# A two-layer decode kernel: the last two heads of each round written apart, two more wo pieces loaded last in round one, ReLU into two PSUM banks

## The chip, the cores and the metric

The kernel runs on one core of a Trainium2 chip. The metric is the device time of one execution in microseconds (us); the time before is the median of three runs. The profile is of one further execution on the same kind of core.

## The reference

Four sequences (B = 4) decode one token. A residual stream x of 4 x 640 goes twice through the same two layers, so the kernel has two rounds:

```python
x = x + _A_ref(_layernorm(x), k_cache, v_cache, wq, wo)   # 32 heads of 128, the last 1024 keys
x = x + _B_ref(_layernorm(x), w1, w2)                     # relu(x @ w1) @ w2, 1728 hidden
x = x + _A_ref(_layernorm(x), k_cache, v_cache, wq, wo)
x = x + _B_ref(_layernorm(x), w1, w2)
```

In `_A_ref` each head computes q = x wq, scores q k / sqrt(128), a softmax over 1024 keys, p v, and adds its part times wo. Everything is float32. Nothing can be shared between the sequences in the attention, since each has its own cache, so per round all keys and values of 32 heads are read once.

## The kernel before, in words

**Data.** The host packs one *record* per head, 128 partitions x 9472 columns: wq (640 columns), keys (4096), values (4096), wo (640) at the column offsets WQ, K, V, WO (line 47). A record is 4.85 MB. It is loaded into one of five SBUF buffers, `slot0` to `slot4`; a sixth buffer, `ring`, holds w1 and w2 of round one and then parts of the first records of round two. Heads 27 to 31 stay in the five slots at the end of round one, and round two begins with them, so that they are read from HBM once.

**Order of the transfers.** All loads go to the SP queue in one list, `items`, built at lines 180 to 216. `pump` (line 218) issues the head of the list as soon as nothing live overlaps its columns; `done` (line 239) frees columns when PE's last use of them has been written down in the program. `ending` (line 170) cuts the records of the last three heads a, b, c of a round into pieces: query weights and keys of a and b, values of a, keys of c, values of b, the values of c in two halves. In round one the three wo pieces of a, b, c are loaded behind all of these (lines 175 to 177, LATE = 3 at line 68), then the five blocks of w1 and seven pieces of w2. The second piece of w2 lies on the columns of the first block of w1, so it cannot be issued before PE has read that block; the same holds for the pieces after it.

**The work of a head** (lines 391 to 405). The engines' programs are written down in order, and each engine runs its own list in that order:
- `query` (291): five 128 x 128 products into the PSUM tile misc, copied by DVE to qT.
- `scores` (298): eight products of 512 columns into sc_ps[s], two banks of PSUM; s alternates by head. DVE takes the maximum, ACT the exponential with its sum.
- `weights` (311): DVE turns that sum into a factor, and transposes and scales the two halves of the exponentials into wT, one after the other.
- `values` (321): eight products of 512 columns, four for each half of the keys, into o_ps, one bank; then DVE picks the right block of each sequence out of o_ps in four operations, into `on`.
- `output_T` (332): PE transposes `on` into the same o_ps, DVE copies it to oTs.
- `project` (336): four products with wo, added into acc.

The loop writes scores of head n+1, then values of head n, the query of head n+2, output and projection of head n, and weights of head n+1. For the last `late` heads of a round (3 in round one, 1 in round two) the projection stands after the loop (lines 406 to 411), because their wo comes last; the last head's output is transposed there too, behind two fillers. A *filler* is `busy(n)` (line 256), a product of n columns into one row of a bank, whose result nobody reads.

**The MLP** (343). `center` (260) makes the layernorm's mean with fillers in between. w1 is multiplied in five blocks into h_ps, the first bank of sc_ps[0], again with fillers. DVE clears 32 columns of h_ps, ACT applies ReLU in three pieces within that bank, and DVE transposes the two halves to `scratch` (355 to 362). The w2 products go into acc tile by tile; the first 28 of the 54 tiles use only the first transposed half.

Of the kernel before, what the change touches and what calls it, by code (L numbers as in the profile page):

```python
# [33 lines left out]
AF = mybir.ActivationFunctionType  # L34
OP = mybir.AluOpType
# [4 lines left out]
B, D, H, DH, W, FF = 4, 640, 32, 128, 1024, 1728  # L40
# [6 lines left out]
WQ, K, V, WO = 0, D, D + 4 * W, D + 8 * W  # L47
REC = 2 * D + 8 * W
# [4 lines left out]
FQ = FF // NB  # L53
# [11 lines left out]
           (7808, 8320, 0)]  # L65
W1_SLOT = [[0, 1], [2], [3], [4]]
W2_SLOT = [22, 20, 8, 4]
LATE = 3


class InOrder:
# [21 lines left out]
def decode_kernel(ctx: ExitStack, tc: tile.TileContext, xf, rec, w1, w2, out):  # L93
    nc = tc.nc
    pe, dve, act, pool, sp = (InOrder(tc, e) for e in (nc.tensor, nc.vector, nc.scalar, nc.gpsimd, nc.sync))
# [3 lines left out]
    mean_of = sb.tile([P, P], F32, name="mean_of")  # L99
    xT = sb.tile([P, FD], F32, name="xT")  # L100
    scratch = sb.tile([P, 480], F32, name="scratch")
    wT = scratch[:, :128].rearrange("p (i c j) -> p i c j", i=2, c=16)
    on = scratch[:, 128:256]
    xc = scratch[:, 256:256 + FD]
    x_sb = scratch[:, :FD]
    spread = scratch[:, 256:288]
    hT = scratch.rearrange("p (m j) -> p m j", j=32)
    oTs = sb.tile([P, LATE, B], F32, name="oTs")
    qT = sb.tile([P, B], F32, name="qT")
    of_batch = sb.tile([P, B], F32, name="of_batch")  # L110
    of_block = sb.tile([P, 4], F32, name="of_block")
    pick = sb.tile([P, B], F32, name="pick")
    mrt = sb.tile([P, B], F32, name="mrt")
    small = sb.tile([P, 12], F32, name="small")
    nmax, rtot, rstd, eps, eps_dh, ones, unused, sums, squares, tot0, tot1 = (small[:, i:i + 1] for i in range(11))
    tot = [tot0, tot1]
    slot = [sb.tile([P, REC], F32, name=f"slot{i}") for i in range(NS)]
    ring = sb.tile([P, RING], F32, name="ring")

    sc_ps = [ps.tile([P, W], F32, name=f"sc_ps{i}") for i in range(2)]  # L120
    t_ps = ps.tile([P, 512], F32, name="t_ps")
    o_ps = ps.tile([P, 512], F32, name="o_ps")
    acc = ps.tile([P, 512], F32, name="acc")
    misc = ps.tile([P, 512], F32, name="misc")

    dve.memset(x_sb, 0.0)
    for n in range(NB):
# [25 lines left out]
    LAST = H - NS  # L153

    def home(h, r):

        return h % NS if not r or h >= LAST else (h - 6 + LAST) % NS
# [6 lines left out]
    def load(key, src, lo, hi, buf, col):  # L164
        items.append((key, src, lo, hi, buf, col))

    def piece(r, h, lo, hi, buf=None, col=None):
        load(("rec", r, h), rec[h], lo, hi, home(h, r) if buf is None else buf, lo if col is None else col)

    def ending(r, hs, late):  # L170
        a, b, c = hs[-3:]
        end = WO if late else REC
        for h, lo, hi in ((a, 0, V), (b, 0, V), (a, V, end), (c, 0, V), (b, V, end), (c, V, V + VH), (c, V + VH, end)):
            piece(r, h, lo, hi)
        if late:
            for h in hs[-3:]:
                piece(r, h, WO, REC)


    hs = order[0]  # L180
    piece(0, hs[0], 0, V)
    piece(0, hs[0], V, REC)
    for h in hs[1:-3]:
        piece(0, h, 0, REC)
    ending(0, hs, True)
    for k, col in enumerate(W1_RING):
        load(("w1", 0), w1, k * FF, k * FF + FF, "ring", col)
    n = 0
# [5 lines left out]
    hs = order[1]  # L194
# [18 lines left out]
    n = 0  # L213
# [39 lines left out]
        pump()  # L253


    def busy(n):

        pe.matmul(sc_ps[1][0:1, :n], mean_of[:, 0:1], slot[home(LAST, 0)][:, K:K + n], start=True, stop=True)

    def center(fill):  # L260

# [26 lines left out]
    def xblock(k):  # L288
        return xT[:, 32 * k:32 * k + B]

    def query(r, h):
        key = ("rec", r, h)
        for k in range(KB):
            pe.matmul(misc[:, 8:8 + B], cols(key, WQ + k * DH, DH), xblock(k), start=(k == 0), stop=(k == KB - 1))
        done(key, WQ, K)
        dve.tensor_copy(qT, misc[:, 8:8 + B])

    def scores(r, h, s, first=False):
        key = ("rec", r, h)
        for i in range(2):  # L300
            for b in range(B):
                pe.matmul(sc_ps[s][32 * b:32 * b + 4, 512 * i:512 * i + 512], qT[:, b:b + 1].to_broadcast([P, 4]),
                          cols(key, K + 512 * (B * i + b), 512), start=True, stop=True)
            done(key, K + VH * i, K + VH * i + VH)
        dve.tensor_reduce(nmax, sc_ps[s], op=OP.max, axis=AX.X, negate=True)
        if first:
            dve.reciprocal(rstd, rstd)
        dve.tensor_tensor(nmax, nmax, rstd, op=OP.mult)
        act.activation(sc_ps[s], sc_ps[s], AF.Exp, bias=nmax, scale=rstd, accum_out=tot[s])

    def weights(s):

        dve.transpose(spread, tot[s].to_broadcast([P, 32]))
        dve.reciprocal(rtot, spread[:, 0:1])
        dve.tensor_scalar(mrt, of_batch, rtot, None, op0=OP.mult)
        for i in range(2):
            dve.transpose(t_ps, sc_ps[s][:, 512 * i:512 * i + 512])
            dve.tensor_tensor(wT[:, i], t_ps.rearrange("p (c j) -> p c j", j=32)[:, :, :B],
                              mrt.unsqueeze(1).to_broadcast([P, 16, B]), op=OP.mult)

    def values(r, h):
        key = ("rec", r, h)
        for i in range(2):
            for g in range(4):
                pe.matmul(o_ps[32 * g:32 * g + 16, :], wT[:, i, 4 * g:4 * g + 4, :].rearrange("p c j -> p (c j)"),
                          cols(key, V + VH * i + 512 * g, 512), start=(i == 0), stop=(i == 1))
            done(key, V + VH * i, V + VH * i + VH)
        dve.tensor_scalar(on, o_ps[:, :DH], of_block[:, 0:1], None, op0=OP.mult)
        for c in range(1, 4):
            dve.scalar_tensor_tensor(on, o_ps[:, DH * c:DH * c + DH], of_block[:, c:c + 1], on, op0=OP.mult, op1=OP.add)  # L330

    def output_T(i):
        pe.matmul(o_ps[:, :B], on, pick, start=True, stop=True)
        dve.tensor_copy(oTs[:, i], o_ps[:, :B])

    def project(r, h, i, end):
        key = ("rec", r, h)
# [3 lines left out]
        done(key, WO, REC)  # L341

    def mlp(r):
        h_ps = sc_ps[0][:, :512]
        for k in range(KB):
            for j in range(NB):
                pe.matmul(h_ps[32 * j:32 * j + B, :FQ], xblock(k), cols(("w1", r), k * FF + FQ * j, FQ),
                          start=(k == 0), stop=(k == KB - 1))
            done(("w1", r), k * FF, k * FF + FF)
            if k == 0:  # L350
                scale_hidden()
            elif k < KB - 1:
                busy(512)

        dve.memset(h_ps[:, FQ:FQ + 32], 0.0)
        act.activation(h_ps[:, :224], h_ps[:, :224], AF.Relu, scale=rstd)
        act.activation(h_ps[:, 464:480], h_ps[:, 416:FQ], AF.Relu, scale=rstd)
        act.activation(h_ps[:, 224:FQ], h_ps[:, 224:FQ], AF.Relu, scale=rstd)
        busy(512)
        busy(256)  # L360
        dve.transpose(scratch[:, :224], h_ps[:, :224])
        dve.transpose(scratch[:, 224:], h_ps[:, 224:480])
        key = ("w2", r)
        sizes = W2_SLOT if r else [size for size, _ in W2_RING]
        first = 0
        for i, size in enumerate(sizes):
            for s in range(first, first + size):
                m, n = TILES[s]
                w = cols(key, s * FD, FD)
                for part, q in ((m, n),) if m < 13 else ((13, n), (14, n + 2)):  # L370
                    pe.matmul(acc[32 * q:32 * q + B, :FD], hT[:, part, :B], w,
                              start=False, stop=(s >= len(TILES) - NB), skip_group_check=True)
            for _ in range((i < len(sizes) - 1, 2 * (i == 0))[r]):
                busy(512)
            done(key, first * FD, (first + size) * FD)
            first += size
# [3 lines left out]
    pe.matmul(acc[:, :FD], ident, x_sb, start=True, stop=False, skip_group_check=True)  # L380
    for r in range(2):
        hs = order[r]
        late = LATE if r == 0 else 1
        center(r > 0)
        dve.tensor_scalar(mrt, mean_of[:, :B], squares, None, op0=OP.mult)
        query(r, hs[0])
        scale_scores()
        scores(r, hs[0], 0, True)
        query(r, hs[1])
        weights(0)  # L390
        for n, h in enumerate(hs):
            more = n + 1 < H
            i = n - (H - late)
            if more:
                scores(r, hs[n + 1], (n + 1) % 2)
            values(r, h)
            if n + 2 < H:
                query(r, hs[n + 2])
            if i < 0:
                output_T(0)  # L400
                project(r, h, 0, False)
            elif more:
                output_T(i)
            if more:
                weights((n + 1) % 2)
        for i in range(late):
            if i == max(0, late - 2):
                busy(512)
                busy(512)
                output_T(late - 1)  # L410
            project(r, hs[H - late + i], i, i == late - 1)
        center(True)
        mlp(r)
# [40 lines left out]
```

## Time and profile before

| | before |
|---|---|
| median of three runs | 727.33 us (726.65 to 728.99) |
| the profiled execution | 727.87 us, its span 726.2 us |
| transfers | 304.49 MB, mean 419 GB/s |
| PE (matmul) busy | 526.8 us, 73% |
| DVE busy | 357.2 us, 49% |
| ACT busy | 96.0 us, 13% |
| mean granted clock of TensorE | 0.788 |

Times in the rows below are us from the span's start. PE is TensorE's matmuls, PEld its weight loads, DVE VectorE, ACT ScalarE, SPq the queue of SyncE that issues the transfers. In a timeline row stand start, duration, engine, line, operation, out<-in, shapes and count; a float32 matmul shows as two. Since a helper records every instruction, all rows have the line L85, and one goes by the tiles' names. The bracket at the end of a row is the idle time of the engine before it and what ended it.

### The profile page before, as it was taken

What the parts mean: (1) busy time and instruction counts of PE and PEld (TensorE: products, weight loads), DVE (VectorE), ACT (ScalarE), POOL (GpSimd) and SP (SyncE); (2) the same over time, 40 slices, a digit from 0 to 9 for tenths busy, and PEclk for the clock granted to TensorE, in tenths of its full rate; (3) what the DMA queues carried; (4) which work ended last, traced back from release to release, by engine and by line L of the source; (5) the groups of instructions that cost most, each with busy time, mean ns of one, the idle gap of its engine ahead of it and who ended that gap; (6) DMA issues with size and microseconds to landing.
All of it is one profiled execution on the core that took longest, in us unless ns stands there. A gap on an engine that the chain in (4) does not pass through costs nothing.

```text
span 726.2 us, 8920 instructions
## 1 busy us (share of the span) xinstructions
PE 526.8 (73%) x3712; PEld 213.4 (29%) x3712; DVE 357.2 (49%) x1000; ACT 96.0 (13%) x154; POOL 1.1 (0%) x9
## 2 busy tenths in 40 slices
PE   3466768677767586668889889675767767768888
PEld 2132322323313232233324343233222232323412
DVE  3344445444454445445732777653444544544750
ACT  2101011010110101101211221210101010110201
POOL 0000000000000000000000000000000000000000
PEclk9778776776687868767999898977787886766969
DMA  9999999999999999999999999999999999999994
GB/s 385 430 425 429 432 433 433 435 431 431 432 431 432 429 431 428 427 427 426 419 361 405 394 423 429 436 430 433 431 432 431 433 430 427 434 429 420 423 422 205
DMA packets 15336, 304.49 MB, mean 419 GB/s; under 512 B 1712, under 2 KB 1984, under 8 KB 5312
## 3 DMA queue, kind: packets, MB, share of 16 engines
q1 hardware_dynamic: 15264, 303.91, 98.3%
q8 instruction: 29, 0.48, 0.3%
q14 instruction: 11, 0.09, 0.0%
q10 hardware_dynamic: 32, 0.01, 0.0%
HBM read 303.84 MB, written 0.08 MB: 419 GB/s over the span
## 4 chain that ended last, share of the span: by engine, by line
DMA 74%; PE 20%; DVE 4%; issue 1%; ACT 0%; SPq 0%
DMA slot<-rec 74%; PE sc_ps L85 8%; PE o_ps L85 5%; PE misc L85 4%; PE acc L85 4%; DVE scratch L85 2%; DVE oTs L85 1%; ACT sc_ps L85 0%; DVE small L85 0%; DVE t_ps L85 0%; SPq L85 0%; DVE mrt L85 0%; SPq L82 0%; DVE sc_ps L85 0%; DVE qT L85 0%
## 5 line engine op out<-in xcount | busy, mean ns | idle before, releaser
L85 PE MATMUL misc<-xT,slot 128*128 128x4 f32 x620 | 102.8, 293 | 154.9 <-DMA slot<-rec 154.0
L85 PE MATMUL sc_ps<-slot,qT 128*4 128x512 f32 x992 | 196.7, 934 | 0.8 <-DVE qT L85 0.7
L85 PEld LDWEIGHTS misc<-xT,slot 128*128 128x128 f32 x620 | 97.4, 242 | 210.7 <-DMA slot<-rec 199.1
L85 ACT ACTIVATE sc_ps<-sc_ps,small 128x1024 f32<-128x1024 f32 (+3 forms) x70 | 77.5, 1107 | 571.8 <-DVE small L85 546.7
L85 PE MATMUL o_ps<-slot,scratch 128*16 128x512 f32 x1010 | 140.1, 673 | 4.3 <-DVE scratch L85 3.5
L85 DVE TENSOR_REDUCE small<-sc_ps 128x1 f32<-128x1024 f32 x64 | 78.2, 1223 | 79.2 <-PE sc_ps L85 79.2
L85 DVE STREAM_TRANSPOSE t_ps<-sc_ps 128x512 f32<-128x512 f32 x128 | 93.2, 728 | 2.2
L85 DVE COPY qT<-misc 128x4 f32<-128x4 f32 x64 | 10.2, 159 | 167.5 <-PE misc L85 167.5
L85 PEld LDWEIGHTS o_ps<-slot,scratch 128*16 128x16 f32 x1010 | 34.1, 117 | 132.2 <-issue 81.2
L85 DVE SCALAR_TENSOR_TENSOR scratch<-o_ps,of_block,scratch 128x128 f32<-128x128 f32 x192 | 67.3, 350 | 6.8
L85 PEld LDWEIGHTS sc_ps<-slot,qT 128*4 128x4 f32 x992 | 33.8, 116 | 84.8 <-issue 74.3
L85 PE MATMUL acc<-slot,oTs 128*4 128x160 f32 x512 | 39.1, 390 | 15.5 <-DVE oTs L85 15.5
L85 DVE TENSOR_SCALAR scratch<-o_ps,of_block 128x128 f32<-128x128 f32 x64 | 22.4, 350 | 38.0 <-PE o_ps L85 38.0
L85 PE MATMUL o_ps<-pick,scratch 128*128 128x4 f32 x128 | 29.4, 300 | 9.4 <-DVE scratch L85 9.4
L85 DVE TENSOR_TENSOR scratch<-t_ps,mrt 128x64 f32<-128x64 f32 x128 | 28.8, 225 | 4.4
L85 PEld LDWEIGHTS o_ps<-pick,scratch 128*128 128x128 f32 x128 | 26.1, 253 | 14.3 <-DVE scratch L85 13.3
L85 PE MATMUL sc_ps<-slot,mean_of 128*1 128x512 f32 (+1 forms) x62 | 28.9, 571 | 0.0
L85 DVE COPY oTs<-o_ps 128x4 f32<-128x4 f32 x64 | 10.4, 162 | 18.6 <-PE o_ps L85 17.5
L85 DVE TENSOR_SCALAR mrt<-of_batch,small 128x4 f32<-128x4 f32 x64 | 14.7, 230 | 2.2
L85 PEld LDWEIGHTS acc<-slot,oTs 128*4 128x4 f32 x512 | 7.3, 84 | 22.1 <-DVE oTs L85 21.0
L85 DVE STREAM_TRANSPOSE scratch<-small 128x32 f32<-128x32 f32 x64 | 12.9, 201 | 1.4 <-ACT sc_ps L85 1.4
L85 ACT ACTIVATION_READ_ACCUMULATOR sc_ps<-sc_ps,small 128x1 f32 x64 | 12.2, 191 | 0.0
(55 smaller groups left out, 104.4 us busy)
## 6 DMA issues: line engine op xcount, KB each, us to landing
slot<-rec SPq DMA_DIRECT2D x46, 4736.0 KB, 30.8
slot<-rec SPq DMA_DIRECT2D x17, 2368.0 KB, 16.9
slot<-rec SPq DMA_DIRECT2D x5, 1024.0 KB, 32.4
ring<-w SPq DMA_DIRECT2D x5, 864.0 KB, 13.6
slot<-rec SPq DMA_DIRECT2D x2, 2048.0 KB, 42.8
slot<-rec SPq DMA_DIRECT2D x3, 1344.0 KB
slot<-w SPq DMA_DIRECT2D x3, 864.0 KB, 31.2
ring<-rec SPq DMA_DIRECT2D x1, 2368.0 KB
```

Source lines behind the costliest of these rows:

```text
L85: r = build(*args, **kwargs)
```

## The change

1. **Loads.** LATE is 5: in round one the wo pieces of the last five heads, not of the last three, come behind the last values. Heads 27 and 28 lose their 640 wo columns in their first load, and two loads of 640 columns are added ahead of the other three.
2. **Last two heads apart.** The loop stops at the third head from the end. Then come the scores of the last head, the values of the head before it, the *weights* of the last head, the picks of the head before it, the values of the last head, its picks. The last head's values, output and picks use a second bank, the upper half of sc_ps[0], and a second `on`.
3. **Fillers.** The two fillers of 512 columns behind the last values go. After each half of the values of the last head but one stands one filler, after each half of the last head's values two, all into misc.
4. **Projections.** In round one five projections stand after the loop, three of them without a transposition between; in round two there are two instead of one.
5. **ReLU.** The first piece goes to t_ps, the other two to the upper bank of sc_ps[0], in the order 208 columns, 16 columns. The memset of the gap stands at the start of the MLP.

```diff
-LATE = 3
+LATE = 5
-    on = scratch[:, 128:256]
+    on = [scratch[:, 128:256], scratch[:, 288:416]]
+    outs = [o_ps, sc_ps[0][:, 512:]]
-            for h in hs[-3:]:
+            for h in hs[-LATE:]:
                 piece(r, h, WO, REC)
-        piece(0, h, 0, REC)
+        piece(0, h, 0, REC if h < H - LATE else WO)
...
-    def values(r, h):
+    def values(r, h, last=False, fill=0):
         key = ("rec", r, h)
         for i in range(2):
             for g in range(4):
-                pe.matmul(o_ps[32 * g:32 * g + 16, :], wT[:, i, 4 * g:4 * g + 4, :].rearrange("p c j -> p (c j)"),
+                pe.matmul(outs[last][32 * g:32 * g + 16, :], wT[:, i, 4 * g:4 * g + 4, :].rearrange("p c j -> p (c j)"),
                           cols(key, V + VH * i + 512 * g, 512), start=(i == 0), stop=(i == 1))
             done(key, V + VH * i, V + VH * i + VH)
+            for _ in range(fill):
+                busy(512, misc)
...
-        h_ps = sc_ps[0][:, :512]
+        h_ps, front, back = sc_ps[0][:, :512], t_ps[:, :224], sc_ps[0][:, 512:768]
+        dve.memset(back[:, 208:240], 0.0)
...
-        dve.memset(h_ps[:, FQ:FQ + 32], 0.0)
-        act.activation(h_ps[:, :224], h_ps[:, :224], AF.Relu, scale=rstd)
-        act.activation(h_ps[:, 464:480], h_ps[:, 416:FQ], AF.Relu, scale=rstd)
-        act.activation(h_ps[:, 224:FQ], h_ps[:, 224:FQ], AF.Relu, scale=rstd)
+        act.activation(front, h_ps[:, :224], AF.Relu, scale=rstd)
+        act.activation(back[:, :208], h_ps[:, 224:FQ], AF.Relu, scale=rstd)
+        act.activation(back[:, 240:], h_ps[:, 416:FQ], AF.Relu, scale=rstd)
...
-        late = LATE if r == 0 else 1
+        late = LATE if r == 0 else 2
...
+        scores(r, hs[-1], 1)
+        values(r, hs[-2], 0, 1)
+        weights(1)
+        picks(0)
+        values(r, hs[-1], 1, 2)
+        picks(1)
         for i in range(late):
-            if i == max(0, late - 2):
-                busy(512)
-                busy(512)
-                output_T(late - 1)
+            if i >= late - 2:
+                output_T(i, i == late - 1)
             project(r, hs[H - late + i], i, i == late - 1)
```

On PE at the end of round two the order was this (slot_72 holds the last head but one, slot_73 the last; sc_ps_77 and sc_ps_78 are sc_ps[0] and sc_ps[1]; rows with mean_of are fillers, rows with pick the transpositions):

```order
L85 MATMUL sc_ps_78<-slot_73,qT 4x512 x8
L85 MATMUL o_ps<-slot_72,scratch 16x512 x8
L85 MATMUL o_ps<-pick,scratch 128x4
L85 MATMUL acc<-slot_72,oTs 4x160 x4
L85 MATMUL o_ps<-slot_73,scratch 16x512 x8
L85 MATMUL sc_ps_78<-slot_73,mean_of 1x512 x2
L85 MATMUL o_ps<-pick,scratch 128x4
L85 MATMUL acc<-slot_73,oTs 4x160 x4
```

Now the same place on PE reads:

```order
L85 MATMUL o_ps<-slot_72,scratch 16x512 x4
L85 MATMUL misc<-slot_73,mean_of 1x512
L85 MATMUL o_ps<-slot_72,scratch 16x512 x4
L85 MATMUL misc<-slot_73,mean_of 1x512
L85 MATMUL sc_ps_77<-slot_73,scratch 16x512 x4
L85 MATMUL misc<-slot_73,mean_of 1x512 x2
L85 MATMUL sc_ps_77<-slot_73,scratch 16x512 x4
L85 MATMUL misc<-slot_73,mean_of 1x512 x2
L85 MATMUL o_ps<-pick,scratch 128x4
L85 MATMUL acc<-slot_72,oTs 4x160 x4
L85 MATMUL sc_ps_77<-pick,scratch 128x4
L85 MATMUL acc<-slot_73,oTs 4x160 x4
```

Output and projection of the head before moved behind the last head's values, and six fillers stand between and behind the halves of the values where two stood at the end.

On DVE in the same stretch (first two rows: picks of the head before; from scratch<-small on: weights of the last head) the order was:

```order
L85 TENSOR_SCALAR scratch<-o_ps,of_block 128x128
L85 SCALAR_TENSOR_TENSOR scratch<-o_ps,of_block,scratch 128x128 x3
L85 COPY oTs<-o_ps 128x4
L85 STREAM_TRANSPOSE scratch<-small 128x32
L85 RECIPROCAL small<-scratch 128x1
L85 TENSOR_SCALAR mrt<-of_batch,small 128x4
L85 STREAM_TRANSPOSE t_ps<-sc_ps_78 128x512
L85 TENSOR_TENSOR scratch<-t_ps,mrt 128x64
```

and DVE's order is now:

```order
L85 STREAM_TRANSPOSE scratch<-small 128x32
L85 RECIPROCAL small<-scratch 128x1
L85 TENSOR_SCALAR mrt<-of_batch,small 128x4
L85 STREAM_TRANSPOSE t_ps<-sc_ps_78 128x512
L85 TENSOR_TENSOR scratch<-t_ps,mrt 128x64
L85 STREAM_TRANSPOSE t_ps<-sc_ps_78 128x512
L85 TENSOR_TENSOR scratch<-t_ps,mrt 128x64
L85 TENSOR_SCALAR scratch<-o_ps,of_block 128x128
L85 SCALAR_TENSOR_TENSOR scratch<-o_ps,of_block,scratch 128x128 x3
L85 TENSOR_SCALAR scratch<-sc_ps_77,of_block 128x128
L85 SCALAR_TENSOR_TENSOR scratch<-sc_ps_77,of_block,scratch 128x128 x3
L85 COPY oTs<-o_ps 128x4
```

The weights of the last head stand ahead of the picks of the head before, and both copies of the outputs behind the last picks. The weights now reuse wT while the values of the head before may still be read from it, so their two products wait for the two halves of those values on PE.

More of the change, by code (lines that the diff above doesn't have):

```diff
@@ L253, in done, with busy @@
         pump()
-    def busy(n):
-        pe.matmul(sc_ps[1][0:1, :n], mean_of[:, 0:1], slot[home(LAST, 0)][:, K:K + n], start=True, stop=True)
+    def busy(n, to=sc_ps[1]):
+        pe.matmul(to[0:1, :n], mean_of[:, 0:1], slot[home(LAST, 0)][:, K:K + n], start=True, stop=True)
     def center(fill):
@@ L324, in values, with picks, output_T @@
             for g in range(4):
-                pe.matmul(o_ps[32 * g:32 * g + 16, :], wT[:, i, 4 * g:4 * g + 4, :].rearrange("p c j -> p (c j)"),
+                pe.matmul(outs[last][32 * g:32 * g + 16, :], wT[:, i, 4 * g:4 * g + 4, :].rearrange("p c j -> p (c j)"),
                           cols(key, V + VH * i + 512 * g, 512), start=(i == 0), stop=(i == 1))
             done(key, V + VH * i, V + VH * i + VH)
-        dve.tensor_scalar(on, o_ps[:, :DH], of_block[:, 0:1], None, op0=OP.mult)
+            for _ in range(fill):
+                busy(512, misc)
+    def picks(last):
+        o, on_ = outs[last], on[last]
+        dve.tensor_scalar(on_, o[:, :DH], of_block[:, 0:1], None, op0=OP.mult)
         for c in range(1, 4):
[L330 to L334, printed above, removed]
+            dve.scalar_tensor_tensor(on_, o[:, DH * c:DH * c + DH], of_block[:, c:c + 1], on_, op0=OP.mult, op1=OP.add)
+    def output_T(i, last=False):
+        pe.matmul(outs[last][:, :B], on[last], pick, start=True, stop=True)
+        dve.tensor_copy(oTs[:, i], outs[last][:, :B])
     def project(r, h, i, end):
@@ L353, in mlp @@
                 busy(512)
-        dve.memset(h_ps[:, FQ:FQ + 32], 0.0)
-        act.activation(h_ps[:, :224], h_ps[:, :224], AF.Relu, scale=rstd)
-        act.activation(h_ps[:, 464:480], h_ps[:, 416:FQ], AF.Relu, scale=rstd)
-        act.activation(h_ps[:, 224:FQ], h_ps[:, 224:FQ], AF.Relu, scale=rstd)
+        act.activation(front, h_ps[:, :224], AF.Relu, scale=rstd)
+        act.activation(back[:, :208], h_ps[:, 224:FQ], AF.Relu, scale=rstd)
+        act.activation(back[:, 240:], h_ps[:, 416:FQ], AF.Relu, scale=rstd)
         busy(512)
         busy(256)
-        dve.transpose(scratch[:, :224], h_ps[:, :224])
-        dve.transpose(scratch[:, 224:], h_ps[:, 224:480])
+        dve.transpose(scratch[:, :224], front)
+        dve.transpose(scratch[:, 224:], back)
         key = ("w2", r)
@@ L390, in decode_kernel @@
         weights(0)
-        for n, h in enumerate(hs):
-            more = n + 1 < H
+        for n, h in enumerate(hs[:-2]):
             i = n - (H - late)
-            if more:
-                scores(r, hs[n + 1], (n + 1) % 2)
+            scores(r, hs[n + 1], (n + 1) % 2)
             values(r, h)
-            if n + 2 < H:
-                query(r, hs[n + 2])
+            picks(0)
+            query(r, hs[n + 2])
+            output_T(max(i, 0))
             if i < 0:
-                output_T(0)
                 project(r, h, 0, False)
[L402 to L405, printed above, removed]
+            weights((n + 1) % 2)
+        scores(r, hs[-1], 1)
+        values(r, hs[-2], 0, 1)
+        weights(1)
+        picks(0)
+        values(r, hs[-1], 1, 2)
+        picks(1)
         for i in range(late):
-            if i == max(0, late - 2):
-                busy(512)
-                busy(512)
-                output_T(late - 1)
+            if i >= late - 2:
+                output_T(i, i == late - 1)
             project(r, hs[H - late + i], i, i == late - 1)
```

## The prediction

> **What bounds the kernel now.** I read the page's slices and its chain first, then the two places where the transfer rate falls, by windows, and then the timeline there.
>
> ```profile
> PEclk9778776776687868767999898977787886766969
> GB/s 385 430 425 429 432 433 433 435 431 431 432 431 432 429 431 428 427 427 426 419 361 405 394 423 429 436 430 433 431 432 431 433 430 427 434 429 420 423 422 205
> DMA 74%; PE 20%; DVE 4%; issue 1%; ACT 0%; SPq 0%
> ```
>
> Transfers carry 74% of the chain that ended last, at about 430 GB/s in nearly every slice. A change can win only where that rate falls: in slices 20 to 22 (the end of round one and the start of round two) and in the last slice, after the weights have landed. The windows show the middle (columns: busy time by engine, granted clock, DMA share, GB/s), the SP rows what was issued in it.
>
> ```profile
> 364.00:368.00 4.00, 2.58 (x20) 0.60 (x24) 2.22 (x7) 0.00 (x0) 0.00 (x0) 0.86 1.03 417
> 372.00:376.00 4.00, 3.97 (x34) 1.39 (x26) 1.23 (x4) 1.97 (x4) 0.00 (x0) 1.00 0.68 276
> 376.00:380.00 4.00, 4.00 (x32) 0.92 (x28) 0.00 (x0) 0.00 (x0) 0.00 (x0) 1.00 0.98 324
> 380.00:384.00 4.00, 3.36 (x26) 0.83 (x22) 0.83 (x3) 1.08 (x3) 0.00 (x0) 1.00 0.97 366
> 408.00:412.00 4.00, 4.00 (x28) 0.72 (x19) 2.48 (x5) 0.60 (x1) 0.00 (x0) 0.60 0.93 378
> 412.00:416.00 4.00, 3.33 (x32) 2.07 (x32) 3.00 (x11) 0.69 (x2) 0.00 (x0) 0.83 1.00 359
> ```
> ```profile
> 375.19 3.04 SPq L85 DMA_DIRECT2D ring<-w  x3
> ```
> ```profile
> 409.86 0.33 SPq L85 DMA_DIRECT2D slot<-rec  x1
> ```
>
> Against 417 GB/s, the three windows from 372 lose 4 x (141 + 93 + 51) / 417 = 2.7 us of transfer, the two from 408 lose 0.9 us. In the first dip w2 cannot be loaded until PE has read w1 block by block, which it starts when the attention of round one is done: the first such load is issued at 375.19. In the second, the load of 409.86 waits for a head of round two. Both dips are PE being late, so what PE gains before them shortens them. At the end PE is late again:
>
> ```profile
> 716.00:720.00 4.00, 3.39 (x58) 1.53 (x59) 0.75 (x2) 0.92 (x3) 0.00 (x0) 1.00 0.29 115
> 720.00:724.00 4.00, 3.17 (x67) 1.60 (x65) 0.32 (x1) 0.00 (x0) 0.00 (x0) 1.00 0.02 4
> ```
> ```profile
> 723.25 0.32 DVE L85 COPY scratch<-acc 128x160 f32<-128x160 f32 x1 [5.49 <-PE acc L85]
> ```
>
> The last weights land before 720 and PE works on until the copy at 723.25, so about 3 us can be won there before the landing itself is the bound.
>
> **Part 1: the end of round two.** Here the change reorders the last two heads. What is there now:
>
> ```profile
> 687.02 1.69 PE L85 MATMUL misc<-xT,slot 128*128 128x4 f32 x10 [1.89 <-DMA slot<-rec]
> 693.29 2.52 PE L85 MATMUL o_ps<-slot,scratch 128*16 128x512 f32 x16
> 696.22 0.19 ACT L85 ACTIVATION_READ_ACCUMULATOR sc_ps<-sc_ps,small 128x1 f32 x1
> 697.95 0.20 DVE L85 STREAM_TRANSPOSE scratch<-small 128x32 f32<-128x32 f32 x1
> 699.56 3.61 PE L85 MATMUL o_ps<-slot,scratch 128*16 128x512 f32 x16 [0.76 <-DVE scratch L85]
> 700.31 0.23 DVE L85 TENSOR_TENSOR scratch<-t_ps,mrt 128x64 f32<-128x64 f32 x1
> 702.95 2.80 PE L85 MATMUL sc_ps<-slot,mean_of 128*1 128x512 f32 x4
> 703.24 0.35 DVE L85 TENSOR_SCALAR scratch<-o_ps,of_block 128x128 f32<-128x128 f32 x1 [2.71 <-PE o_ps L85]
> 703.63 1.12 DVE L85 SCALAR_TENSOR_TENSOR scratch<-o_ps,of_block,scratch 128x128 f32<-128x128 f32 x3
> 705.67 0.39 PE L85 MATMUL o_ps<-pick,scratch 128*128 128x4 f32 x2
> 706.84 0.33 DVE L85 TENSOR_REDUCE small<-acc 128x1 f32<-128x160 f32 x1 [0.58 <-PE acc L85]
> ```
> ```profile
> 696.00:700.00 4.00, 1.54 (x14) 0.55 (x18) 3.28 (x11) 0.41 (x2) 0.00 (x0) 0.74 1.00 423
> 700.00:704.00 4.00, 4.00 (x18) 0.67 (x11) 1.20 (x4) 0.00 (x0) 0.00 (x0) 0.50 0.99 410
> ```
>
> The sum of the softmax is ready at 696.41, but DVE is still picking the blocks of the head before and begins the weights at 697.95, 1.5 us later. PE, almost idle meanwhile (1.54 of 4 us), gets the half clock, and the last values take 3.61 us.
>
> In the changed order the weights start at about 696.5. Their first half is ready 1.6 us later (699.56 less 697.95), at 698.1, their second at 699.1 (697.95 to 700.54 is 2.6). The picks of the head before run behind them on DVE until 700.6. On PE the values before get two fillers of 512 columns. At full clock half of a head's values takes 0.9 (the row of 359.77 below: 16 in 1.91) and a filler 0.9 too (the row of 715.42 below: one of 512 and one of 256 in 1.45). The first half runs at half clock until about 694.8; filler, half, filler end at 697.5, before 698.1, so these fillers cost nothing: the wait for the weights hides them. The last head's values with two fillers behind each half are on the path: 698.1 + 0.9 + 1.8 + 0.9 + 1.8 = 703.5. The middle 1.8 delays the second half past its weights (699.1) by 1.7; the last 1.8 covers the picks (0.35 + 1.12, about 1.5 us from 701.7) but ends 0.3 later. Then two times transposition, copy and projection, 1.1 each (from 705.67 to just short of 706.84): 705.7. Against 706.84 this gains 1.2, **if the clock is full** through the last head. The fillers make PE 80% busy from 694.5 to 698, as in the windows from 372 to 380, where the clock was 1.00. If the clock stays at half for all of it, the 5.4 us double. Without the middle fillers' cost the gain would be about 2.5. The two windows now hold 2 x 0.26 x 4 + 4 = 6.1 us of half clock; half as much, 3.3, under the changed head would cost 1.65. Bounds: -0.5 (with that) to +2.
>
> [...]
>
> **Part 2: ReLU.** Now the memset and three ReLU pieces in one bank come ahead of the first transposition:
>
> ```profile
> 715.42 1.45 PE L85 MATMUL sc_ps<-slot,mean_of 128*1 128x512 f32 x4
> 715.84 1.14 ACT L85 ACTIVATE sc_ps<-sc_ps,small 128x224 f32<-128x224 f32 x3 [5.52 <-DVE sc_ps L85]
> 717.01 0.75 DVE L85 STREAM_TRANSPOSE scratch<-sc_ps 128x224 f32<-128x224 f32 x2 [1.21 <-ACT sc_ps L85]
> 717.48 1.80 PE L85 MATMUL acc<-slot,scratch 128*4 128x160 f32 x44 [0.61 <-DVE scratch L85]
> ```
> ```profile
> 715.84 0.43 ACT sc_ps L85
> 717.01 0.43 DVE scratch L85
> ```
>
> DVE waits for all three pieces and transposes at 717.01. With the memset at the start of the stage (DVE is free there) and the first piece in another bank, t_ps, the chain is one piece and one transposition: 715.74 (the memset's tenth earlier) + 0.43 + 0.43, with two short hand-overs 716.65. PE's own fillers end at 716.87, issue allowing at 716.7. So the first w2 product moves from 717.48 to 716.7: 0.8 us, at least 0.6, in each round. The other half (0.3 later on DVE) is first read after 28 tiles; at 44 products in 1.80 these are 2.3 us and cover it.
>
> **Part 3: the end of round one.** The same reordering, and two more wo pieces behind the last values:
>
> ```profile
> 332.33 0.90 PE L85 MATMUL misc<-xT,slot 128*128 128x4 f32 x5 [1.79 <-DMA slot<-rec]
> ```
> ```profile
> 359.77 1.91 PE L85 MATMUL o_ps<-slot,scratch 128*16 128x512 f32 x16 [0.80 <-DMA slot<-rec]
> 362.39 0.19 ACT L85 ACTIVATION_READ_ACCUMULATOR sc_ps<-sc_ps,small 128x1 f32 x1
> 365.42 2.57 PE L85 MATMUL o_ps<-slot,scratch 128*16 128x512 f32 x16 [1.72 <-DVE scratch L85]
> 372.24 0.32 DVE L85 TENSOR_REDUCE small<-acc 128x1 f32<-128x160 f32 x1 [0.58 <-PE acc L85]
> ```
>
> Each piece is 128 x 640 x 4 bytes, 0.33 MB, 0.8 us at 417 GB/s, so keys and values of the last heads land up to 1.6 us earlier. PE waited for them (332.33, 359.77), so its work moves by 1.6: the exponential ends at 361.0 instead of 362.58, the weights come at 362.7, the last head ends at 362.7 + 5.4 = 368.1. But now three projections stand behind it where one did before it: 3 x 0.5, then 2 x 1.1, gives 371.7 against 372.24: a gain of 0.5. Bounds: -1.2 (3.3 us at half clock) to +1.6 (the whole shift). The two extra DMAs are issued by SP ahead of the w1 loads and wait for nothing late, since their columns are long free; the bytes stay the same.
>
> What a small transfer costs beside its bytes is bounded by this row and the window of 364 above:
>
> ```profile
> slot<-rec SPq DMA_DIRECT2D x4, 320.0 KB, 5.5
> ```
>
> From issue to landing it takes 5.5 us, of which the bytes are 0.8. If nothing of the rest overlapped, two would cost 9.4. But the window 364 to 368, in which the three present ones pass, ran at share 1.03 and 417 GB/s, so I take 0. [...]
>
> **The sum.** Round one: 0.5 + 0.8 = 1.3 us on PE. The first dip takes the 0.5, the second (0.9 lost) the 0.8, and round two, bound by transfers, ends 1.3 earlier. End: 1.2 + 0.8 = 2.0. Together 3.3. The profiled execution took 727.87 (span 726.2 and 1.7 around it): 724.6. It lies 0.5 above the median of 727.33, so I forecast **724.0**.
>
> **Rivals.**
> - *The middle is not passed on* (chance 0.2): the queue of transfers stays short, and only the end gains, 2.0: 725.3. For it: windows 376 to 384 show a DMA share of 0.97 and more at low rate. Against: each load there is issued on a PE event.
> - *Half clock under the longer last head* (0.12): the place is PE between the last weights and the projections, where values and four fillers, 5.4 us per round, would run at 0.5. In full, 10.8 - 3.3 = 7.5 slower: 734.8. It decides at 3.3 us of half clock per round: 1.65 twice uses up the 3.3 and leaves 727.3; beyond that the change loses. For it: the half clock from 700 to 704 while PE was fully busy. Against: that followed a slack stretch, which the fillers now fill. I give 0.06 to each. [...]
> - *Small transfers are not overlapped* (0.03): 9.4 us in round one, less 3.3: 733.4.
> - *The banks don't decouple* (0.05), DVE still waits for ACT: 3.3 - 1.6 = 1.7, 725.6.
> - *More* (0.1): upper bounds 1.6, 2.0 and 0.9 twice: 5.4, 721.9.
>
> **How the numbers follow.** The forecast has 0.5. A measurement tells 0.3%, 2.2 us, from no change: under 725.15 is faster. That holds for the forecast, for *more*, and for half of the first rival: 0.7. The rest of it, 3.3 us of half clock, the banks and a little of the transfers make 0.22 the same, the remainder 0.08 slower. The range runs from 721.9 to 726.5, a gain of only 0.8; beyond it lie the clock rival and the transfers.
>
> **What would show it.** Right: weights straight behind the last exponential; a clock near 1.0 through the last values; the centring reduction 0.5 and 1.2 us closer to the arrivals than now; the first transposition 0.5 after the first ReLU piece; the dips at 372 to 384 and at 411 shallower. Wrong: a clock of 0.5 under the last values, a dip as deep as before, or a DVE wait for all of ReLU.

## The result and the profile after

The changed kernel takes 718.71 us (717.67 to 719.46, four runs) against 726.99 for the kernel before on the same chip. The ratio is 0.9881, 95% interval 0.9855 to 0.9906: 8.3 us faster, more than twice the 3.3 of the forecast, and below its range. The profiled execution took 719.46, its span 717.7.

The same slices and the chain of the page, of the changed kernel:

```profile
PEclk9778686876676777677999999878668786767989
GB/s 379 433 436 434 439 432 421 433 438 435 436 430 422 434 438 435 435 417 434 420 407 415 425 430 431 442 432 433 430 431 436 436 431 428 434 433 424 426 428 237
DMA 75%; PE 20%; DVE 3%; issue 1%; ACT 0%; SPq 0%
```

Slices 20 to 22 dip much less (407, 415, 425 where there were 361, 405, 394). And something stands there that nothing in the prediction speaks of: slices far from any edited line are faster too. One long window in round one and one in round two show it best, here of the kernel before:

```profile
40.00:300.00 260.00, 181.04 (x1186) 73.35 (x1178) 123.74 (x340) 29.80 (x46) 0.00 (x0) 0.75 1.00 430
460.00:640.00 180.00, 121.81 (x840) 50.62 (x832) 88.41 (x246) 22.02 (x34) 0.00 (x0) 0.77 1.00 431
```

and here of the changed one (last column GB/s):

```profile
40.00:300.00 260.00, 184.82 (x1200) 75.01 (x1196) 125.42 (x346) 29.79 (x46) 0.00 (x0) 0.74 1.00 433
460.00:640.00 180.00, 124.93 (x816) 51.31 (x816) 85.69 (x239) 20.72 (x32) 0.00 (x0) 0.74 1.00 433
```

The DMA share is 1.00 in all four: the transfers never wait, they only run 0.5 to 0.7% faster. On 304 MB, some 700 us, that is about 3 us or more.

The windows of the two dips, of the changed kernel:

```profile
372.00:376.00 4.00, 4.00 (x36) 0.92 (x28) 0.11 (x1) 0.00 (x0) 0.00 (x0) 1.00 0.98 367
376.00:380.00 4.00, 4.00 (x40) 1.27 (x37) 0.87 (x2) 1.08 (x3) 0.00 (x0) 1.00 1.01 420
380.00:384.00 4.00, 4.00 (x59) 1.85 (x60) 0.00 (x0) 0.00 (x0) 0.00 (x0) 1.00 1.01 410
408.00:412.00 4.00, 3.75 (x41) 1.00 (x40) 3.72 (x10) 0.00 (x0) 0.00 (x0) 1.00 0.99 421
412.00:416.00 4.00, 3.32 (x36) 2.03 (x36) 3.16 (x13) 1.29 (x2) 0.00 (x0) 1.00 1.03 438
```
```profile
371.38 4.63 SPq L85 DMA_DIRECT2D ring<-w  x4
```

Against 417 GB/s the first dip now loses 4 x 50 / 417 = 0.5 us where it lost 2.7, and the second is gone. Against the rate of the long windows (431 before, 433 now) slices 20 to 22 lost 18.2 x (70 + 26 + 37) / 431 = 5.6 us before and still lose 17.9 x (26 + 18 + 8) / 433 = 2.2 us. The first w2 load that waits for PE is issued at 371.38 instead of 375.19, 3.8 us earlier.

The end of round two, timeline of the changed kernel:

```profile
680.78 1.28 PE L85 MATMUL misc<-xT,slot 128*128 128x4 f32 x10 [2.01 <-DMA slot<-rec]
686.48 1.91 PE L85 MATMUL o_ps<-slot,scratch 128*16 128x512 f32 x8 [0.81 <-DMA slot<-rec]
688.36 0.19 ACT L85 ACTIVATION_READ_ACCUMULATOR sc_ps<-sc_ps,small 128x1 f32 x1
688.59 0.21 DVE L85 STREAM_TRANSPOSE scratch<-small 128x32 f32<-128x32 f32 x1 [1.44 <-ACT sc_ps L85]
697.10 0.38 PE L85 MATMUL o_ps<-pick,scratch 128*128 128x4 f32 x2
699.28 0.33 DVE L85 TENSOR_REDUCE small<-acc 128x1 f32<-128x160 f32 x1 [0.58 <-PE acc L85]
```
```profile
684.00:688.00 4.00, 3.19 (x16) 0.30 (x9) 2.33 (x4) 0.74 (x1) 0.00 (x0) 0.50 1.01 427
688.00:692.00 4.00, 4.00 (x23) 0.89 (x19) 2.91 (x9) 0.55 (x2) 0.00 (x0) 0.70 1.01 431
692.00:696.00 4.00, 4.00 (x20) 0.82 (x15) 1.24 (x5) 0.00 (x0) 0.00 (x0) 1.00 1.00 422
```

The weights now follow the exponential at once: its sum is ready at 688.55 and they begin at 688.59. From the arrival of the last keys to the centring reduction it takes 18.50 us (680.78 to 699.28) where it took 19.82 (687.02 to 706.84): 1.3 less, where 1.2 was forecast. ReLU and the first w2 product:

```profile
707.87 1.45 PE L85 MATMUL sc_ps<-slot,mean_of 128*1 128x512 f32 x4
708.12 0.42 ACT L85 ACTIVATE t_ps<-sc_ps,small 128x224 f32<-128x224 f32 x1 [5.36 <-PE sc_ps L85]
708.58 0.42 DVE L85 STREAM_TRANSPOSE scratch<-t_ps 128x224 f32<-128x224 f32 x1 [5.61 <-ACT t_ps L85]
709.05 1.22 PE L85 MATMUL acc<-slot,scratch 128*4 128x160 f32 x28
```

From the last filler group to the product there are 1.18 us (707.87 to 709.05) where there were 2.06 (715.42 to 717.48): 0.88 less, 0.8 was forecast.

### The profile page after: what moved, and what is told of

Same layout as the page of the kernel before. It is cut to its first block, busy times and chain, and to the rows that moved or that the text cites. A ratio compares the mean times of both kernels' runs of the same rounds, so it can differ in the third digit from the quotient of the medians.

```text
span 717.7 us, 8963 instructions
## 1 busy us (share of the span) xinstructions
PE 531.5 (74%) x3728; PEld 214.0 (30%) x3728; DVE 357.9 (50%) x1000; ACT 96.0 (13%) x154; POOL 1.1 (0%) x9
## 4 chain that ended last, share of the span: by engine, by line
DMA 75%; PE 20%; DVE 3%; issue 1%; ACT 0%; SPq 0%
DMA slot<-rec 75%; PE sc_ps L85 7%; PE misc L85 5%; PE o_ps L85 4%; PE acc L85 4%; DVE scratch L85 2%; DVE oTs L85 1%; DVE small L85 0%; DVE t_ps L85 0%; ACT sc_ps L85 0%; SPq L85 0%; SPq L82 0%; DVE mrt L85 0%; DVE qT L85 0%
## 5 line engine op out<-in xcount | busy, mean ns | idle before, releaser
L85 PE MATMUL sc_ps<-slot,qT 128*4 128x512 f32 x992 | 194.1, 923 | 0.9 <-DVE qT L85 0.7
L85 ACT ACTIVATE sc_ps<-sc_ps,small 128x1024 f32<-128x1024 f32 (+1 forms) x68 | 76.6, 1127 | 553.5 <-DVE small L85 547.1
L85 DVE SCALAR_TENSOR_TENSOR scratch<-o_ps,of_block,scratch 128x128 f32<-128x128 f32 x186 | 65.3, 351 | 6.6
L85 PE MATMUL sc_ps<-slot,mean_of 128*1 128x512 f32 (+1 forms) x54 | 23.2, 529 | 0.0
L85 PE MATMUL misc<-slot,mean_of 128*1 128x512 f32 x24 | 12.5, 631 | 0.0
```

Of the source, the lines that this page charges most:

```text
L85: r = build(*args, **kwargs)
```

## The experiments

All times below, other than those read from a trace, are medians beside the kernel before on the same chip (726.8 to 727.0 there).

### What else does LATE set? The address of the slots

LATE is also the length of oTs (line 108): `oTs = sb.tile([P, LATE, B], F32)`. Five entries take 32 bytes per partition more than three after rounding, and the slots and the ring are allocated behind it. In the kernel before slot0 starts at byte 3552 of a partition, in the changed one at 3584; every slot is 37888 bytes long, a multiple of 512, so all of them share the remainder. Theory A is that this address sets the rate of the transfers; theory B, the rival, that it is drift or one of the edits. The lines below are one edit of each run:

```diff
-    oTs = sb.tile([P, LATE, B], F32, name="oTs")
+    oTs = sb.tile([P, 5, B], F32, name="oTs")       # e1_align, on the kernel before
+    oTs = sb.tile([P, 7, B], F32, name="oTs")       # e4_shift32, on the changed kernel
+    oTs = sb.tile([P, 9, B], F32, name="oTs")       # e5_shift64
+    oTs = sb.tile([P, 14, B], F32, name="oTs")      # e9_shift128
+    oTs = sb.tile([P, 22, B], F32, name="oTs")      # e10_shift256
```

> The kernel before, with oTs made five entries long instead of three and nothing else: the five slots and the ring then start 32 bytes later in each partition, at 3584 instead of 3552. Theory A (the start address sets the rate of the transfers): the faster rate of the changed kernel, about 0.4% in all stretches that no edit touches, comes with it; 2.7 to 3.5 us faster than before, 723.5 to 724.3. Theory B (drift from run to run, or something in the edits): no change within 0.7 us.

Measured: 722.79 (719.59 to 724.33), ratio 0.9931 (0.9912 to 0.9950): 4.2 us faster with the same instructions, more than the 2.7 to 3.5 that theory A expected. Theory B is out. The first long window of e1_align has the changed kernel's rate:

```profile
40.00:300.00 260.00, 180.38 (x1196) 73.66 (x1188) 124.16 (x344) 29.81 (x46) 0.00 (x0) 0.76 1.00 433
```

> The changed kernel with oTs padded to seven entries: the slots start at 3616, 32 bytes past a multiple of 64. Theory A: the transfers lose their rate again, 2.7 to 3.5 us slower than the changed kernel, 721.4 to 722.2. Theory B: as fast as the changed kernel, 718.7.

Measured: 722.76 (722.71 to 724.16), ratio to before 0.9946 (0.9933 to 0.9960): 4.1 us slower than the changed kernel, with its whole program. The rate is the old one:

```profile
40.00:300.00 260.00, 183.95 (x1196) 74.77 (x1196) 125.01 (x345) 29.80 (x46) 0.00 (x0) 0.74 1.00 431
```

So the address is worth about 4 us in both directions, and **the edits by themselves about 4.3** (727.03 to 722.76; by the interval 2.9 to 4.9).

> The changed kernel with oTs padded to nine entries: the slots start at 3648, a multiple of 64 but not of 128 or more (3584 is a multiple of 512). If a multiple of 64 bytes is what the transfers want: as fast as the changed kernel, 718.7. If they want 128 to 512: about 4 us slower, as e4_shift32, 722.8.

Measured: 722.02 (721.97 to 724.20). 3648, a multiple of 64, has the slower rate: 431 GB/s from 40 to 300.

> The changed kernel with oTs padded so that the slots start at 3712, a multiple of 128 but not of 256. e5_shift64 (3648) was slow, 722.0. If a multiple of 128 is enough: 718.7. If 256 or 512 is wanted: about 722.

Measured: 721.77 (721.68 to 722.21). 3712, a multiple of 128, has it too: 431 GB/s in the same window.

> The changed kernel with the slots at 3840, a multiple of 256 but not of 512. If 256 is enough: 718.7; if only 512 is: about 722. If it is not the remainder but the one address 3584: 722 as well.

Measured: 720.08 (717.64 to 720.74), two of the six runs at 717.6 and 718.0, and none as slow as the shifts by 32, 64 and 128 (721.7 and more). The window from 40 to 300 runs at 433 GB/s here and at 431 in e5_shift64 and e9_shift128:

```profile
40.00:300.00 260.00, 184.20 (x1212) 74.96 (x1216) 125.85 (x350) 29.78 (x46) 0.00 (x0) 0.74 1.00 433
```

So 3840, a multiple of 256 but not of 512, has the rate of 3584; the medians, 720.1 against 718.7, don't settle whether 3584 gives another bit, but the traces show none (180 to 300 MB in the table further below: 278.4 us here, 278.1 to 278.5 at 3584). Of the six addresses tried, the two that are multiples of 256 run at 433 GB/s from 40 to 300 and the four others at 430 to 431. Why the address matters is not shown.

Does it need the computation beside it? Two kernels leave all of that out; the one at 3584 also has the longer oTs (excerpt):

```diff
...
+    for n in range(59):
+        s = slot[n % NS]
+        sp.dma_start(s, rec[n % H])
+        dve.tensor_tensor(small[:, 0:1], small[:, 0:1], s[:, 0:1], op=OP.add)
...
```

> A kernel that leaves out all the computation: 59 whole records loaded into the five slots at the old address 3552, one small DVE addition for each, no PE. 286 MB; at the 430 to 431 GB/s that the kernel before shows in stretches without a dip 664 to 665 us, and some 10 us around it. Theory A: slower than e12_loads_3584 by 0.4 to 0.7%, 3 to 4.5 us. Theory C (the address matters only through PE's or DVE's reads that meet the transfers): no difference between the two.

> The same loads without the computation, slots at 3584. Theory A: at 433 GB/s, 0.4 to 0.7% faster than e11_loads_3552, 3 to 4.5 us. Theory C: the same time.

Measured: 671.41 (671.30 to 671.65) at 3552 and 668.93 (668.90 to 669.21) at 3584. The window, first at 3552:

```profile
40.00:300.00 260.00, 3.67 (x23) 0.00 (x0) 1.00 1.00 432
```

and at 3584:

```profile
40.00:300.00 260.00, 3.67 (x23) 0.00 (x0) 1.00 1.00 434
```

2.5 us, 0.37%, and the runs don't overlap: the transfers alone show it, theory C is out. The size is just under theory A's 3 to 4.5. Scaled to 304 MB it is 2.6 us, less than the 4 of the whole kernels. The packets of their traces show where more comes from. The seven kernels at a multiple of 256 have the first 155 MB delivered at 361.9 to 362.1, the five others at 363.3 to 363.7: 1.5 in the mean. From 180 to 300 MB (table below) it is another 1.4, whatever the edits. In the stretch between, which holds both dips, pairs that differ in the address alone (before and e1_align, e4_shift32 and the changed kernel) differ by 0.6. Together 3.5; the rest, about half a microsecond, is within the intervals.

### The edits, one by one

> The kernel before with five wo pieces last instead of three (which makes oTs five entries long as well, so the slots move as in e1_align). Theory A with the shift of the arrivals passed on (1.6 us): 1 to 2 us faster than e1_align, 722 to 723. Theory B and the prediction's step (three projections behind the last head eat the gain of 1.6): within 0.7 us of e1_align.

```diff
-LATE = 3
+LATE = 5
-            for h in hs[-3:]:
+            for h in hs[-LATE:]:
-        piece(0, h, 0, REC)
+        piece(0, h, 0, REC if h < H - LATE else WO)
```

Measured: 720.81 (719.81 to 721.68), 2.0 faster than e1_align at the same addresses, though the runs of the two overlap (e1_align has one at 719.59). The traces agree with a gain: the last query of round one starts 1.6 us earlier (351.15 instead of 352.74), and the stretch of the dips is 1.2 shorter (62.8 instead of 64.0, table below).

> The changed kernel with three wo pieces last instead of five, slots at the same addresses as the changed kernel. Theory A' (the earlier arrivals pass on in full, as e2_late5 against e1_align showed 2.0): 2 us slower than the changed kernel, 720.7. The prediction's step (three projections behind the last head eat most of the 1.6): at most 0.5 slower, 719.2.

```diff
-LATE = 5
+LATE = 3
-    oTs = sb.tile([P, LATE, B], F32, name="oTs")
+    oTs = sb.tile([P, 5, B], F32, name="oTs")
```

Measured: 719.79 (719.15 to 722.28), 1.1 slower than the changed kernel: between the two theories, with runs that just overlap. In the traces the stretch of the dips is 2.0 longer (62.5 against 60.5). With e2_late5 the wo pieces are worth 1 to 2 us.

> The kernel before with ReLU into two banks alone, slots where they were. 0.6 to 0.9 us per round on PE, and passed on to the transfers in round one: 1.3 to 1.7 us faster than before, 725.3 to 725.7. If the transfers don't take the first round's share: 0.8 us.

Its edit is part 5 of the change. Measured: 724.33 (723.44 to 725.27), ratio 0.9964 (0.9951 to 0.9977), 2.7 faster, of which the interval leaves 1.7 to 3.6, where 1.3 to 1.7 was expected. The transfers do take round one's share; more than 1.7 is not proved. The traces account for about 1.4: in round two the first w2 product comes 9.77 us after the centring reduction in all seven traces with the new ReLU other than e6_nofill (below), 10.65 in all four with the old one, and the stretch of the dips is 0.5 shorter here than before.

> The kernel before with the last two heads written apart and the fillers alone, ReLU and the three late wo pieces as before, slots at 3584 as in e1_align (722.8). By the prediction: 1.2 at the end and something in round one, together 1.5 to 3 us faster than e1_align, 720 to 721.3. Rival: alignment (4.2), wo pieces (2.0) and ReLU (2.7) already add up to 8.9, more than the 8.3 of the whole change, so this part brings nothing: 722.8 within 0.7.

Its edit is the changed kernel with LATE = 3, the old ReLU and oTs of five entries. Measured: 722.00 (720.78 to 723.87), 0.8 faster than e1_align, with overlapping runs: inconclusive between 1.5 and nothing. The traces say more than the times. Each row is one profiled execution. The two columns of MB are the us from the delivery of that many megabytes to the other, by the packets of the load queue: 155 to 180 MB holds both dips, 180 to 300 MB none. The last two are the us from the start of the last head's query product to the centring reduction, with the granted clock of that stretch in brackets.

| profiled execution | slots at | order of the heads | 155 to 180 MB | 180 to 300 MB | round one | round two |
|---|---|---|---|---|---|---|
| before | 3552 | old | 64.6 | 279.7 | 17.2 (0.90) | 19.8 (0.66) |
| e3_relu | 3552 | old | 64.0 | 279.7 | 18.6 (0.74) | 17.6 (0.90) |
| e1_align | 3584 | old | 64.0 | 278.4 | 17.2 (0.90) | 19.8 (0.65) |
| e2_late5 | 3584 | old | 62.8 | 278.1 | 17.8 (0.90) | 17.7 (0.90) |
| e8_heads | 3584 | new | 63.9 | 278.2 | 18.6 (0.82) | 16.6 (1.00) |
| e7_late3 | 3584 | new | 62.5 | 278.5 | 17.0 (1.00) | 17.5 (0.90) |
| changed kernel | 3584 | new | 60.5 | 278.3 | 17.1 (1.00) | 18.5 (0.82) |
| e10_shift256 | 3840 | new | 60.9 | 278.4 | 17.0 (1.00) | 16.6 (1.00) |
| e4_shift32 | 3616 | new | 61.2 | 280.0 | 17.1 (1.00) | 16.6 (1.00) |
| e5_shift64 | 3648 | new | 61.2 | 279.7 | 17.6 (0.90) | 16.6 (1.00) |
| e9_shift128 | 3712 | new | 61.1 | 279.6 | 17.0 (1.00) | 16.6 (1.00) |
| e6_nofill (below) | 3584 | new, no fillers | 60.9 | 278.2 | 17.0 (0.70) | 15.4 (1.00) |

In round two the old order takes 17.6 to 19.8, the new one with its fillers 16.6 to 18.5: means of 18.7 and 17.0, 1.7 gained. The length goes with the granted clock: at 0.90 the old order takes 17.6 and 17.7, the new one 17.5. The gain is that the new order got the full clock in five of its seven traces and the old one in none of its four. Programs with the same order spread by 2 us here, which is the size of what is looked for. On the dips the order alone brings nothing (63.9 against 64.0), and the single edits there (0.1, 1.2 for the wo pieces, 0.5 for ReLU) are less than the 3.4 of all together; why is open. The medians don't add up either: 4.2 + 2.0 + 2.7 + 0.8 = 9.7, more than the 8.3 of the whole change.

> The changed kernel without the six fillers in the last two heads of a round. By the prediction's working the clock falls to half for the last values (3.4 us instead of 5.4 with full clock and fillers), the end comes 0.4 us earlier or at the same time per round: within 1 us of 718.7. If the fillers are what the order of heads needs: 1 to 2 us per round slower, 720.7 to 722.7. If they are pure cost on the path: 2 to 3 us faster, about 716.

```diff
-        values(r, hs[-2], 0, 1)
+        values(r, hs[-2], 0, 0)
-        values(r, hs[-1], 1, 2)
+        values(r, hs[-1], 1, 0)
```

Measured: 719.02 (718.27 to 721.45) against 718.71: no difference in time. In the trace the fillers both pay and cost. In round one the clock was at 0.70 without them and the stage as long as with them at 1.00 (17.0). In round two the clock held through the last heads without them,

```profile
684.00:688.00 4.00, 3.00 (x34) 0.70 (x28) 3.32 (x7) 0.42 (x1) 0.00 (x0) 1.00 1.00 424
688.00:692.00 4.00, 1.82 (x16) 0.16 (x8) 2.75 (x9) 0.87 (x2) 0.00 (x0) 1.00 1.03 440
692.00:696.00 4.00, 2.14 (x20) 0.86 (x20) 2.45 (x8) 0.00 (x0) 0.00 (x0) 1.00 0.98 413
696.00:700.00 4.00, 3.77 (x19) 1.13 (x23) 1.31 (x5) 1.55 (x3) 0.00 (x0) 0.58 1.04 439
```

with PE about half busy from 688 to 696, and the stage took 15.4, 1.2 less than with fillers at the same clock. It fell in the last of these windows, and from the centring reduction to the first w2 product it then took 11.3 us (696.75 to 708.01) where every other trace with the new ReLU has 9.8: what was saved was lost again.

## Why the prediction was wrong, and where it was right

**What failed: part 3's reading of what LATE changes.** It put down for LATE = 5 two moved wo pieces, "since their columns are long free; the bytes stay the same", and the sum has no other term for it. LATE also lengthens oTs, and that moved every load buffer by 32 bytes onto a multiple of 512. That is 4 us of the 8.3 (e1_align, e4_shift32), half of what was measured, and it acts in the 90% of the span that the prediction took as given: "bound by transfers". No rival held it either; they were about the issue of transfers, the clock and waits between engines, none about how fast the transfers run.

**What failed second: the term of round one, 1.3 us (0.5 + 0.8), was too small.** At equal addresses the edits shorten the stretch of the dips by 3.4 us, from 64.6 to 61.2 (before, e4_shift32) and from 64.0 to 60.5 (e1_align, changed kernel). The prediction thought that only 3.6 us were lost there (2.7 + 0.9), since it counted five windows of 4 us against 417 GB/s, the rate of a window beside them. The three slices against 431 lose 5.6, as worked out above.

**The rest of the sum holds in total, and in part by luck.** At an old kind of address (e4_shift32) the edits gain 4.3 us, 2.9 to 4.9, where 3.3 was forecast. But if 3.4 of that is the dips, the end brings only about 0.9 in the medians, where 2.0 was forecast. The two traces have 2.1 there (from 300 MB delivered to the end of the span 18.2 us before and 16.2 in e4_shift32), but these two executions are 5.1 apart and not 4.3.

- *The end, 2.0*: 1.3 and 0.88 in the profiled execution, close to the forecast 1.2 and 0.8. The 1.3 is luck: it compares one execution at a clock of 0.66 with one at 0.82, and at full clock the new stage takes 16.6, not 18.5. Nor was it by the expected way in each step: PE waited 0.81 us for the values of the last head but one (686.48), the clock was 0.50 from 684 to 688 and 0.70 from 688 to 692, and the first of the fillers ran in that slow stretch. The prediction had these values waiting for nothing and the clock back in time.
- *ReLU, 0.8 in each round*: 0.88 in round two, in every trace; the whole edit alone 2.7, 1.7 to 3.6, of which the traces account for 1.4.
- *Round one, 0.5 for the heads and wo pieces*: mis-sized. The centring reduction comes 3.8 us earlier (372.24 to 368.43, as below), and at equal addresses still 2.2 (370.07 in e4_shift32) or 1.5 (369.94 in e1_align); the wo pieces alone bring 1 to 2 us. In the working (whose last sum, 368.1 + 1.5 + 2.2, is 371.8 and not 371.7) three projections stood wholly behind the last fillers, 5.4 + 1.5 = 6.9 us from the last values' start to the transposition. The timeline of the changed kernel has 6.1 (360.19 to 366.25):

```profile
360.19 1.05 PE L85 MATMUL sc_ps<-slot,scratch 128*16 128x512 f32 x8 [0.34 <-issue]
363.62 1.45 PE L85 MATMUL misc<-slot,mean_of 128*1 128x512 f32 x3
364.49 0.45 PE L85 MATMUL acc<-slot,oTs 128*4 128x160 f32 x6
365.34 0.98 PE L85 MATMUL acc<-slot,oTs 128*4 128x160 f32 x18
366.25 0.38 PE L85 MATMUL o_ps<-pick,scratch 128*128 128x4 f32 x2
368.43 0.32 DVE L85 TENSOR_REDUCE small<-acc 128x1 f32<-128x160 f32 x1 [0.58 <-PE acc L85]
```

  Six products of the first projection run beside the fillers (364.49 within 363.62 + 1.45), and the rest in 0.98. The remainder of the 3.8 is arrivals: 1.6 by the wo pieces, as worked out and as e2_late5 shows, and the faster transfers: by the packets of the two traces the first 155 MB are delivered 1.5 us earlier (362.1 instead of 363.6).
- *The middle passed on*: right, so the first rival falls: the 3.4 us of the dips are still there when 300 MB are delivered, 3.1 at the old kind of address (708.0 to 704.8) and 3.4 at the new (704.3 to 700.9).

**The other rivals.** Half clock under the longer last head did occur in part in the profiled execution (0.50 and 0.70) and cost about 1.9 us there (18.5 at a mean of 0.82, 16.6 at 1.00), less than the change gained; leaving out the fillers it was about makes no difference in time (e6_nofill). Small transfers were overlapped: with two more of them the kernel with five late pieces is no slower than the one with three (720.81 against 722.79, 718.71 against 719.79). With ReLU in two banks DVE did not wait for all of it: at 708.58 ACT begins its other two pieces (0.69 us) and DVE the first transposition (0.42 us).

**The clock.** By the clock's records in the twelve profiles of whole kernels, the granted clock changes only at the borders of stretches of 3.41 us. Behind the first 40 us it falls 610 times, and for 385 of these falls no pause of PE that touches the stretch before is as long as 3.4 us. The prediction took slack as the cause (PE busy 1.54 of 4 us ahead of the half clock). As a condition that is borne out: in the stretch before each fall PE was busy, by its matmul rows, 87% of the time at most, 41% in the median, and in the stretch before each of the 600 rises 90% at least. It does not account for every case: in e6_nofill three stretches in a row, from 686.4 to 696.6, were busy 56, 52 and 52%, and the clock fell only behind the third. The fillers as the remedy are half right: with them the last heads ran at full clock in ten of fourteen stages and with the old order in none of eight, but they take about the time that the clock saves, and without them it was full in one of two. What decides between slack stretches stays open here.

## What to carry to other kernels

When a constant changes, list everything that it sizes, and compare the addresses of all load buffers before and after; where the transfers fill the span as here, try them at a multiple of 256 bytes within the partition (3584 and 3840 ran at 433 GB/s, the four other addresses at 430 to 431), padding the small tiles ahead of them. Look first at the rate in stretches that no edit touches: if it moved, a padded copy of the old kernel tells whether the buffers' address did it, as e1_align does here. When sizing a dip, compare with the rate of long undisturbed windows and not with a window next to the dip. Where a stage shifts by 2 us from trace to trace with the granted clock, as here (the old order in round two 17.6 at 0.90 and 19.8 at 0.65), a single profiled execution can't size an edit of 1 us there; compare several.

## What the runs showed of the hardware that was not expected

- The start address of a load's target within the partition: 3584 and 3840 run at 433 GB/s in the window from 40 to 300, 3552, 3616, 3648 and 3712 at 430 to 431. Loads alone: 668.93 at 3584 against 671.41 us at 3552 for 286 MB.
- Products into another tile started while a filler ran: in the changed kernel six of the first projection start at 364.49 to 364.63, between two starts of fillers at 364.48 and 364.91 that are as far apart as the others (0.43). So these six did not wait for the 0.43 us of the filler ahead of them, nor did they put off the one behind.
